# Two last rows of Y and Z per batch pair in one row-tiled product, made once for all eight batches

## The chip, the cores and the metric

The kernel runs on one core of one Trainium2 chip. The metric is device time in microseconds. TensorE (PE) multiplies, its weight loads are shown as PEld; VectorE is DVE, ScalarE is ACT, GpSimd is POOL, and SyncE is SP. SP, ACT and POOL also issue DMA transfers, which run on the core's 16 DMA engines: queue q0 carries what POOL issues, q1 what SP issues, q10 what ACT issues.

## The reference

Sliding-window attention (8 batches, 8 heads, 576 positions of 64 dimensions, window 64) gives x with 576 rows and 512 columns per batch. Then, per batch:

```python
X = np.fft.rfft(x, axis=1)
Xr, Xi = (np.real(X[:, :n_modes]), np.imag(X[:, :n_modes]))      # 64 modes
Yr = np.einsum('bmd,mde->bme', Xr, w_r) - np.einsum('bmd,mde->bme', Xi, w_i)
Yi = np.einsum('bmd,mde->bme', Xr, w_i) + np.einsum('bmd,mde->bme', Xi, w_r)
Y[:, :n_modes] = Yr + 1j * Yi
y = np.fft.irfft(Y, n=S, axis=1)
u = x + y
return (u + np.maximum(u @ w_ch, 0.0)).astype(np.float32)
```

w_r and w_i have 64 matrices of 512 x 512 each, together 128 MiB in fp32. They are read once.

## The kernel before, in words

**Stages.** POOL issues the loads of q, k, v and of the weights (L165, cast to bf16 on the way, 1 MB as landed). Attention runs under the first half of the weight loads, the products of modes with weights (`mode_half`, L188) under all of them. A group of four modes has four weight loads: two halves of the 512 inputs (hb), each with w_r and w_i (ri). The list `steps` sets their order. The modes of groups LAST = 12 and 13, which give rows 96 to 111 of Y (`rows`, L591, 16 of 128 rows: real and imaginary part of eight modes), come last.

**What is done with Y.** With T the inverse transform as a matrix (`trigI` in bf16, `trigIr` in fp32r, 128 rows of Y by 576 positions), u = x + T Y. The second part is u w_ch = x w_ch + T (Y w_ch) = x w_ch + T Z. The products x w_ch are made under the loads, one per tile of 128 positions, and kept as `XW[i]` (L756). A finished group goes through `finish_group`: `turn` (L648) transposes its staged rows into YT (the tile Yall, seen as transposed). `batch_job(b)` turns that round into rows of Y (`yrows`, tile Yall, ACT, L689) and multiplies it with w_ch into rows of Z (`multiply`, L610; ACT casts it into Zall, L693). Rows 96 to 111 are zero in both until the end.

**Tiles.** There are 36: four per batch of 128 positions each, and four "x4" tiles (8, 17, 26, 35), each of which holds the last 64 positions of two batches. For the 16 tiles of batches 0 to 3 (NLB = 4) `early_u` and `add_late` (L703, L704) add T Y and T Z of the 112 known rows under the loads, into UE[i] and XW[i]; only the 16 last rows remain for the tail. The others take all rows in the tail.

**The order of jobs under the last loads.** `batch_job`, `early_u` and `add_late` are put in one list. `advance` prepares one job and finishes the one before it. The variable `want` sets how many are advanced after each half step, and what is left is done before the last w_r and w_i products of the load stage (`half == n0+n1-2`).

**After the last landing** (L994 to L1023): the last group's rows are staged (`cast_halves`: DVE takes one half, ACT the other). `turn` transposes them; `put_first` (L656) puts the last rows of batches 0 to 3 into one PSUM bank, 32 partitions per batch, for the row-tiled products of the tail; `put_y` (L652) puts all rows of all batches in another. ACT copies `trz` (L663, the transposed rows of batches 0 to 3) and `trl` (L660, all of them). trz times w_ch in two halves (L1007) gives ZL, cast by DVE and ACT. trl times w_ch (L1015) gives the last rows of Z for all batches. Two DMAs carry the last rows into their places: Yall (L1011, from yst) and Zall (L1021, from zst).

**The tail.** `seq` lists pairs of tiles. A pair of early tiles takes `tail_xw` (L786, XW through an identity product), `late_u` (L796) and `late_z` (L803): products with only 16 rows, which sit in separate row groups of TensorE (tile_position), so that a pair's four run side by side. DVE adds into UE (L829), ACT applies the relu (L834), POOL adds both (L835). Other pairs take `full_u` (L845 adds x through an identity product, L849 or, for x4 tiles, L854 adds T Y) and `full_z` (L786, L868 adds T Z with all 128 rows; DVE takes relu and sum, L899). In `add_x` some tiles leave out L845: DVE adds x instead (L860), or POOL (L864). Results go out through SP (L821, in the order of `plan`) and ACT.

**The tables of the row-tiled products** (L950 to L952) are copies of the 16 last rows of trigI and trigIr into four row groups, eight DMAs on SP, made at the start of the second load stage.

```python
r = slice(YG[b], YG[b] + 16)
nc.tensor.matmul(out=pu[i], lhsT=trigL[r, at:at + 128], rhs=YL[r], start=True, stop=True,
                 tile_position=(YG[b], 0))
```

Of the kernel before, what the change touches and what calls it, by code (L numbers as in the profile page):

```python
# [26 lines left out]
def kernel(  # L27
# [39 lines left out]
    ident = consts.tile([128, 128], FP32, name="ident")  # L67
# [3 lines left out]
    pick = consts.tile([128, 32 * NLB + 8], BF16, name="pick")  # L71
# [125 lines left out]
    with tc.manual_schedule():  # L197
        maskp = pool("maskp")
        mask_t = maskp.tile([128, 2, 4, 128], BF16, name="mask_t")
# [221 lines left out]
        def trig_steps():  # L421
            yield lambda: ve.memset(trigF[64:128, NTC - 1, :], 0.0)
            yield lambda: ve.memset(trigF[0:64, NTC, :], 0.0)

            yield lambda: ve.tensor_copy(out=sel, in_=ident.rearrange("p (g x) -> p g x", x=32)[:, :, 0:16])
            yield lambda: ve.memset(pick, 0.0)
            yield lambda: zero_xq(1, ve)
            for to in range(0, NLB, 2):
                b = (to + 2) % NLB
                yield lambda to=to, b=b: ve.tensor_copy(  # L430
                    out=pick[:, 8:].rearrange("p (b x) -> p b x", b=NLB)[:, to:to + 2, 0:8].rearrange("p b (g r) -> p b g r", g=4),
                    in_=sel.rearrange("p g (r b) -> p b g r", b=B)[:, b:b + 2])
# [93 lines left out]
        trigL = zpool.tile([128, 4 * 128], BF16, name="trigL")  # L526
        trigLr = zpool.tile([128, 4 * 128], FP32R, name="trigLr")
        trl = zpool.tile([128, NDCH, 128], FP32R, name="trl")
        trz = zpool.tile([128, NDCH, NLB, 32], FP32R, name="trz")
# [3 lines left out]
        rowpool = pool("rowpool", reuse_waits="tile")  # L533
# [58 lines left out]
        YG, ZG = (64, 96, 0, 32), (0, 32, 64, 96)  # L592
# [37 lines left out]
        def finish_group(grp, psm):  # L630
            stg = stgpool.tile([128, DM], BF16, name="stg")
            if grp == LAST + 1:
                cast_halves(stg, psm)
            elif grp < EARLY:
                nc.vector.tensor_tensor(out=stg, in0=psm, in1=Yacc[grp], op=ALU.add)  # L635
            else:
                nc.vector.tensor_copy(out=stg, in_=psm)
            i = grp % 2
            end = grp - i == LAST
            if i == 0:  # L640
                late["pt"] = bank("p", [128, NDCH, 128])
                late["py"] = bank("y") if end else None
            pt, py = late["pt"], late["py"]
            lanes = sel.rearrange("p g x -> p (g x)")

            def turn():
                for c in range(NDCH):
                    nc.tensor.matmul(out=pt[:, c, 64 * i:64 * i + 64], lhsT=stg[:, 128 * c:128 * c + 128], rhs=lanes,  # L648
                                     start=True, stop=True)

            def put_y():
                nc.tensor.matmul(out=py[64 * i:64 * i + 64, :], lhsT=lanes, rhs=stg, start=True, stop=True,  # L652
                                 tile_position=(0, 64 * i))

            def put_first():
                nc.tensor.matmul(out=late["first"], lhsT=pick[:, 8 - 8 * i:136 - 8 * i], rhs=stg,  # L656
                                 start=(i == 0), stop=(i == 1))

            def take():
                nc.scalar.copy(out=trl[:, :, 64 * i:64 * i + 64], in_=pt[:, :, 64 * i:64 * i + 64])  # L660

            def take_first():
                nc.scalar.copy(out=trz[:, :, :, 8 * i:8 * i + 8],  # L663
                               in_=pt[:, :, 64 * i:64 * i + 64].rearrange("p c (r b) -> p c b r", b=B)[:, :, 0:NLB])

            def prepare():
                turn()
                if end:
                    put_y()
                    take_first()  # L670
                    take()
                elif i:
                    k0 = 8 * (grp - 1)
                    nc.scalar.copy(out=YT[:, :, :, k0:k0 + 16], in_=pt.rearrange("p c (k b) -> p b c k", b=B))

            if end:
                late[i] = turn, put_first, take, put_y, take_first
            if not (end and i):
                ready.append(prepare)
# [19 lines left out]
        def add_late(b, c):  # L699
            def done(_):  # L700
                i = tile_of(b, c)
                pz = bank("z")
                nc.tensor.matmul(out=pz, lhsT=trigIr[:, 128 * c:128 * c + 128], rhs=zrows(b), start=True, stop=True)  # L703
                nc.vector.tensor_tensor(out=XW[i], in0=pz, in1=XW[i].bitcast(FP32), op=ALU.add)  # L704

            jobs.append((lambda: None, done))
# [23 lines left out]
        def early_jobs(b):  # L730
            early_u(b, (1,))
            add_late(b, 0)
            early_u(b, (3,))
            add_late(b, 1)
            add_late(b, 2)
            early_u(b, (0, 2))
            add_late(b, 3)
# [25 lines left out]
        AA = [(18 * k // 2 + c, 18 * k // 2 + 4 + c) for k in range(NLB // 2) for c in range(4)]  # L763
# [28 lines left out]
        def late_u(n):  # L792
            for i in seq[n]:
                (at, b), = tiles[i][1]
                r = slice(YG[b], YG[b] + 16)
                nc.tensor.matmul(out=pu[i], lhsT=trigL[r, at:at + 128], rhs=YL[r], start=True, stop=True,  # L796
                                 tile_position=(YG[b], 0))

        def late_z(n):
            for i in seq[n]:  # L800
                (at, b), = tiles[i][1]
                r = slice(ZG[b], ZG[b] + 16)
                nc.tensor.matmul(out=ps[i], lhsT=trigLr[r, at:at + 128], rhs=ZL[r], start=False, stop=True,  # L803
                                 skip_group_check=True, tile_position=(ZG[b], 0))
# [34 lines left out]
        add_x = {X4[0][1]: "dve", X4[1][0]: "dve", X4[1][1]: "dve", BB[0][0]: "dve", BB[0][1]: "pool"}  # L839
# [26 lines left out]
        def rows_z(i):  # L866
            for at, b in tiles[i][1]:
                nc.tensor.matmul(out=ps[i], lhsT=trigIr[:, at:at + 128], rhs=zrows(b), start=False, stop=True,  # L868
                                 skip_group_check=True)
# [25 lines left out]
        def full_z(n):  # L895
            ut = uts[n]
            for j, i in enumerate(seq[n]):
                rows_z(i)
                nc.vector.scalar_tensor_tensor(out=ut[:, j], in0=ps[i], scalar=0.0, in1=ut[:, j],  # L899
                                               op0=ALU.max, op1=ALU.add)  # L900
                send(i, ut[:, j])
# [34 lines left out]
        for i, (grp, hb) in enumerate(steps[EARLY:]):  # L936
            f, l = grp < EARLY or hb == 0, hb == 1
            if i == EARLY:
                while tables:
                    tables.pop(0)()  # L940
                while jobs or pend:
# [6 lines left out]
                nc.vector.tensor_scalar(out=trz.rearrange("p c g k -> p c (g k)"), scalar1=0.0, scalar2=None, op0=ALU.mult,  # L948
                                        in0=ident.unsqueeze(1).to_broadcast([128, NDCH, 128]))
                for g in range(4):  # L950
                    nc.sync.dma_start(out=trigL[32 * g:32 * g + 16], in_=trigI[rows, 0:512])
                    nc.sync.dma_start(out=trigLr.bitcast(FP32)[32 * g:32 * g + 16], in_=trigIr.bitcast(FP32)[rows, 0:512])  # L952
# [3 lines left out]
            for ri in range(2):  # L956
# [16 lines left out]
                if l and ri:  # L973
                    finish_group(grp, psm)
                    if grp == NGRP - 1:
                        ready.pop(0)()
                        for b in range(B):
                            batch_job(b)
                            if 0 < b <= NLB:
                                early_jobs(b - 1)  # L980
                half += 1
# [4 lines left out]
                else:  # L986
                    want = NT - NX0 + (half - n0 - n1 + 8) * (B + 7 * NLB) * 2 // 11
# [6 lines left out]
        turn, put_first, take, put_y, take_first = late[1]  # L994
        tr, first = trl, late["first"]
        turn()
        take_first()
        put_first()
        put_y()
# [4 lines left out]
        zl = [bank("z"), bank("m")]  # L1004
# [4 lines left out]
        yst = rowpool.tile([128, DM], BF16, name="yst")  # L1009
        nc.scalar.copy(out=yst, in_=late["py"])  # L1010
        nc.sync.dma_start(out=Yall[rows], in_=yst)  # L1011
        cast_halves(ZL, zl)
        pz = bank("p")
        for c in range(NDCH):
            nc.tensor.matmul(out=pz, lhsT=tr[:, c, :], rhs=wch[:, c, :], start=(c == 0), stop=(c == NDCH - 1))  # L1015
        banks_u(0)
        late_u(0)
        late_z(0)
        zst = trpool.tile([128, NDCH, 128], FP32R, name="tr").rearrange("p c k -> p (c k)")
        nc.scalar.copy(out=zst, in_=pz)  # L1020
        nc.sync.dma_start(out=Zall.bitcast(FP32)[rows], in_=zst.bitcast(FP32))  # L1021
        take_u(0)
        take_z(0)  # L1023
        for n in range(1, len(seq) - 1):
# [40 lines left out]
```

## Time and profile before

| what | value |
|---|---|
| median of three runs | 435.41 us (435.04 to 435.62) |
| the profiled execution's own time | 435.39 us |
| its span | 433.6 us |
| PE busy | 327.2 us, 75% |
| DVE busy | 229.8 us, 53% |
| ACT busy | 180.1 us, 42% |
| POOL busy | 101.2 us, 23% |
| q0, software_dynamic | 81.73 MB, 99.7% of 16 engines' span |
| q1, hardware_dynamic | 9.77 MB, 6.6% |
| mean granted TensorE clock | 0.899 |

The span is the time from the first to the last instruction that the profile records. Busy time is the sum of an engine's instructions; TensorE's matmuls are pipelined, so that the start of one and the start of the next say more than the shown duration. Rows of the timeline read: start, microseconds, engine, line, operation, output<-inputs, shapes, count, and in brackets the idle time ahead of it and what ended it. Rows of the chain read: time, duration, engine, output, line.

### The profile page before, as it was taken

The numbers are of one execution on the slowest core, as the hardware profiler recorded it, in microseconds if no ns is written. First come the engines' busy times: TensorE is split into PE (matmuls) and PEld (weight loads), VectorE is DVE, ScalarE is ACT, GpSimd is POOL, SyncE is SP. The second block draws the span as 40 slices with busy tenths as digits, with TensorE's granted clock in tenths as the row PEclk, the third lists the DMA queues.
The fourth block names the chain that finished last, engine by engine and source line by source line (L and its number), as shares of the span: only waits on it lengthen the run. The fifth ranks groups of instructions, "written<-read, shape, count | busy, mean of one in ns | idle before, by whom it ended". The sixth has DMA issues, their size and how long they took to land.

```text
span 433.6 us, 11034 instructions
## 1 busy us (share of the span) xinstructions
PE 327.2 (75%) x4802; PEld 214.6 (49%) x4802; DVE 229.8 (53%) x472; ACT 180.1 (42%) x322; POOL 101.2 (23%) x150
## 2 busy tenths in 40 slices
PE   6999999998999999963208343767584668779993
PEld 3666667576667666641104121444353345445652
DVE  8588787876776776863104111122131325752994
ACT  5665757565666666520201100122121213434842
POOL 8322222222131231122102100012111112110990
PEclk8899999999999999996557768588889989999998
DMA  8999999999999999999999999999999999993798
GB/s 203 212 211 212 211 211 213 210 211 212 212 213 211 212 212 211 212 213 211 212 259 212 218 212 212 212 210 212 212 209 212 211 212 212 212 212 77 245 365 288
DMA packets 47280, 93.64 MB, mean 216 GB/s; under 512 B 2688, under 2 KB 3136, under 8 KB 47232
## 3 DMA queue, kind: packets, MB, share of 16 engines
q0 software_dynamic: 41008, 81.73, 99.7%
q1 hardware_dynamic: 5328, 9.77, 6.6%
q10 hardware_dynamic: 896, 1.44, 0.9%
q8 instruction: 37, 0.61, 0.5%
q14 instruction: 11, 0.09, 0.1%
HBM read 163.58 MB, written 9.44 MB: 399 GB/s over the span
## 4 chain that ended last, share of the span: by engine, by line
DMA 51%; PE 36%; issue 5%; ACT 3%; DVE 3%; POOL 1%; DVEq 0%; POOLq 0%
DMA wi<-in_moe_w_i_dram 29%; DMA wr<-in_moe_w_r_dram 22%; PE tr L231 6%; PE s L278 4%; PE s L270 3%; PE s L290 3%; PE pt L298 3%; PE psm L188 3%; PE vb L243 3%; PE o L318 2%; PE psz L786 1%; PE pst L786 1%; PE pst L868 1%; PE psz L610 1%; PE px L341 1%
## 5 line engine op out<-in xcount | busy, mean ns | idle before, releaser
L610 PE MATMUL psz<-wch,tr 128*128 128x512 f32 x176 | 62.3, 486 | 11.7 <-DMA wch<-in_moe_w_ch_dram 11.0
L756 DVE CAST xw<-psz 128x512 fp32r<-128x512 f32 x36 | 24.9, 692 | 86.1 <-PE psz L610 86.1
L584 ACT CAST tr<-ptx 128x512 fp32r<-128x512 bf16 x36 | 21.1, 586 | 104.1 <-PE ptx L603 104.1
L282 DVE TENSOR_REDUCE mx<-s 128x4 fp32r<-128x512 f32 x72 | 49.6, 688 | 27.0 <-PE s L278 26.7
L188 PEld LDWEIGHTS <-XQ 128*32 128x32 bf16 x448 | 18.8, 175 | 79.2 <-issue 55.9
L188 PE MATMUL psm<-wi,XQ 128*32 128x512 bf16 x208 | 20.1, 461 | 37.6 <-DMA wi<-in_moe_w_i_dram 37.6
L165 POOL DMA_DIRECT2D wi<-in_moe_w_i_dram x32 | 23.4, 732 | 102.8 <-PE psm L188 74.7
L610 PEld LDWEIGHTS psz<-wch,tr 128*128 128x128 f32 x176 | 36.8, 232 | 18.8 <-issue 11.5
L292 ACT ACTIVATE p<-s 128x512 bf16<-128x512 f32 x72 | 39.7, 603 | 12.9 <-PE s L290 12.9
L165 POOL DMA_DIRECT2D wr<-in_moe_w_r_dram x27 | 20.2, 749 | 97.0 <-PE psm L188 49.0
L188 PE MATMUL psm<-wr,XQ 128*32 128x512 bf16 x184 | 17.9, 465 | 28.3 <-DMA wr<-in_moe_w_r_dram 27.4
L235 ACT COPY kT<-tr 128x576 bf16<-128x576 bf16 x32 | 23.2, 724 | 21.1 <-PE tr L231 21.1
L278 PE MATMUL s<-kT,qT 64*64 64x128 bf16 (+1 forms) x576 | 29.2, 221 | 0.0
L270 PE MATMUL s<-mask_t,ident_bf 128*128 128x512 bf16 x72 | 28.4, 395 | 0.9 <-ACT p L292 0.8
L301 DVE COPY pts<-pt 128x1024 bf16<-128x1024 bf16 (+1 forms) x40 | 25.2, 629 | 5.0 <-PE pt L298 3.6
L235 ACT COPY qT<-tr 128x576 bf16<-128x576 bf16 x32 | 23.3, 728 | 10.6 <-PE tr L231 10.6
L278 PEld LDWEIGHTS <-qT 64*64 64x64 bf16 x576 | 17.8, 107 | 18.0 <-issue 17.5
L635 DVE TENSOR_TENSOR stg<-psm,Yfour 128x512 bf16<-128x512 f32 x10 | 6.9, 690 | 36.8 <-PE psm L188 36.8
L290 PE MATMUL s<-mx,ident_r 128*128 128x512 f32 x72 | 26.2, 437 | 0.0
L235 ACT COPY vT<-tr 128x576 bf16<-128x576 bf16 x32 | 23.3, 727 | 4.3 <-PE tr L231 4.2
L298 PE MATMUL pt<-ident_bf,p 128*128 128x128 bf16 x288 | 23.3, 220 | 1.7 <-issue 1.6
L218 POOL DMA_DIRECT2D rawk<-in_k_dram x15 | 8.1, 539 | 65.3 <-PE tr L231 59.1
(217 smaller groups left out, 607.4 us busy)
## 6 DMA issues: line engine op xcount, KB each, us to landing
wi<-in_moe_w_i_dram POOLq DMA_DIRECT2D x29, 1024.0 KB, 18.6
wr<-in_moe_w_r_dram POOLq DMA_DIRECT2D x27, 1024.0 KB, 17.9
out_dram<-ut SPq DMA_DIRECT2D x23, 256.0 KB, 2.8
rawv<-in_v_dram POOLq DMA_DIRECT2D x16, 288.0 KB, 15.0
rawk<-in_k_dram POOLq DMA_DIRECT2D x15, 288.0 KB, 14.1
rawq<-in_q_dram POOLq DMA_DIRECT2D x15, 288.0 KB, 14.0
x_sb<-in_moe_w_r_dram POOLq DMA_DIRECT2D x2, 1024.0 KB, 15.9
out_dram<-utx SPq DMA_DIRECT2D x5, 256.0 KB, 3.1
```

The costliest lines, as they stand in the source:

```text
L165: nc.gpsimd.dma_start(out=w[:, to:to + len(ps)], in_=src[ps[0]:ps[-1] + 1, HALF * hb:HALF * hb + HALF, :].rearrange("g (p j) e -> p g j e" ...
L188: nc.tensor.matmul(out=ps[32 * g:32 * g + 32, 0:e], lhsT=of.rearrange("k s b m -> k (s b) m")[:, (3 * j + 1 - ri) * B:(3 * j + 5 - ri) * B ...
L231: nc.tensor.transpose(out=pt[ro, j, :], in_=raw[ro, TH * half + j, :], identity=ident_bf[ro, ro])
L235: nc.scalar.copy(out=to, in_=pt.rearrange("p j n -> p n j"))
L270: nc.tensor.matmul(out=s, lhsT=ident_bf, rhs=mask_t[:, mk], start=True, stop=True)
L278: nc.tensor.matmul(out=s[ro, t, lo:128], lhsT=lq, rhs=kT[ro, 64 * n - 64 + lo:64 * n + 64], start=False, stop=True, skip_group_check=True)
L282: nc.vector.tensor_reduce(out=mx, in_=s, axis=AX.X, op=ALU.max, negate=True)
L290: nc.tensor.matmul(out=s, lhsT=ident_r, rhs=mx.unsqueeze(2).to_broadcast([128, 4, 128]), start=False, stop=True, skip_group_check=True)
L292: nc.scalar.activation(out=p[:, 4 * c2:4 * c2 + 4, :], in_=s, func=ACT_F.Exp, scale=EX_SCALE)
L298: nc.tensor.transpose(out=pt[:, t, :], in_=st[u]["p"][:, t, :], identity=ident_bf)
L301: nc.vector.tensor_copy(out=ps[:, 0:nt, :], in_=pt[:, 0:nt, :])
L610: nc.tensor.matmul(out=pz, lhsT=tr[:, c, :], rhs=wch[:, c, :], start=(c == 0), stop=(c == NDCH - 1))
```

## The change

- **Last rows for all batches at once.** `put_first` and `turn` now use `pick`, regrouped so that the 16 last rows of *two* batches lie in one group of 32 partitions (four groups for eight batches). One product group then gives YL and ZL for all eight batches. `put_y`, the copies trl and yst, the product L1015 and the cast zst go.
- **Row-tiled products of 32 rows.** trigL and trigLr get a second copy each, with zeros at the rows of the other batch (rows of the two batches alternate), so that a product over 32 rows gives one batch's part. Pairs of early tiles are now of batches b and b + 2, so that the two lie in different row groups.
- **Copies of the last rows.** Four Yall DMAs (two batches each) and two Zall DMAs (batches 4 to 7) from YL and ZL take the place of the two. The Zall rows of batches 0 to 3 stay zero, as nothing reads them after.
- **x4 tiles.** Their T Z of the 112 known rows is added to XW under the loads (four more `add_late`, each of two products). In the tail one product over 32 rows with `trigX`, whose 128 columns hold both batches' tables, adds the rest. Three of the four leave `add_x`: x comes through L845 again, and ACT, not DVE, copies the result.
- **Order after the last landing.** `late_u` of the first pair comes between the two halves of the trz product.
- **Tables.** The copies of trigL, trigLr and trigX are 24 DMAs on SP where there were 8; DVE clears trigL and trigLr first. `pick` is built by six small copies where there were two.

```diff
-            for to in range(0, NLB, 2):
...
+            to = pick[:, 16:].rearrange("p (n x) -> p n x", x=32)[:, :, 0:16]
+            for n in range(6):
+                yield lambda n=n: ve.tensor_copy(
+                    out=to[:, n].rearrange("p (g r b) -> p g r b", g=4, b=2),
+                    in_=sel.rearrange("p g (r n b) -> p n g r b", n=4, b=2)[:, n % 4])
...
-        trl = zpool.tile([128, NDCH, 128], FP32R, name="trl")
-        trz = zpool.tile([128, NDCH, NLB, 32], FP32R, name="trz")
+        trz = zpool.tile([128, NDCH, 4, 32], FP32R, name="trz")
+        trigX = zpool.tile([128, 128], FP32R, name="trigX")
...
+        def group_y(b):
+            return 32 * ((b // 2 + 2) % 4)
+
+        def group_z(b):
+            return 32 * (b // 2)
...
             def take():
-                nc.scalar.copy(out=trl[:, :, 64 * i:64 * i + 64], in_=pt[:, :, 64 * i:64 * i + 64])
-
-            def take_first():
-                nc.scalar.copy(out=trz[:, :, :, 8 * i:8 * i + 8],
-                               in_=pt[:, :, 64 * i:64 * i + 64].rearrange("p c (r b) -> p c b r", b=B)[:, :, 0:NLB])
+                nc.scalar.copy(out=trz[:, :, :, 16 * i:16 * i + 16],
+                               in_=pt[:, :, 64 * i:64 * i + 64].rearrange("p c (g x) -> p c g x", x=16))
...
+        def add_late(i):
             def done(_):
-                i = tile_of(b, c)
                 pz = bank("z")
-                nc.tensor.matmul(out=pz, lhsT=trigIr[:, 128 * c:128 * c + 128], rhs=zrows(b), start=True, stop=True)
+                for n, (at, b) in enumerate(tiles[i][1]):
+                    nc.tensor.matmul(out=pz, lhsT=trigIr[:, at:at + 128], rhs=zrows(b), start=(n == 0),
+                                     stop=(n == len(tiles[i][1]) - 1))
                 nc.vector.tensor_tensor(out=XW[i], in0=pz, in1=XW[i].bitcast(FP32), op=ALU.add)
...
-        AA = [(18 * k // 2 + c, 18 * k // 2 + 4 + c) for k in range(NLB // 2) for c in range(4)]
+        AA = [(tile_of(b, c), tile_of(b + 2, c)) for b in range(NLB // 2) for c in range(4)]
...
-                r = slice(ZG[b], ZG[b] + 16)
-                nc.tensor.matmul(out=ps[i], lhsT=trigLr[r, at:at + 128], rhs=ZL[r], start=False, stop=True,
-                                 skip_group_check=True, tile_position=(ZG[b], 0))
+                r = slice(group_z(b), group_z(b) + 32)
+                nc.tensor.matmul(out=ps[i], lhsT=trigLr[r, b % 2, at:at + 128], rhs=ZL[r], start=False, stop=True,
+                                 skip_group_check=True, tile_position=(group_z(b), 0))
...
-        add_x = {X4[0][1]: "dve", X4[1][0]: "dve", X4[1][1]: "dve", BB[0][0]: "dve", BB[0][1]: "pool"}
+        add_x = {BB[0][0]: "dve", BB[0][1]: "pool"}
...
         def rows_z(i):
-            for at, b in tiles[i][1]:
-                nc.tensor.matmul(out=ps[i], lhsT=trigIr[:, at:at + 128], rhs=zrows(b), start=False, stop=True,
-                                 skip_group_check=True)
+            at, b = tiles[i][1][0]
+            if len(tiles[i][1]) == 2:
+                r = slice(group_z(b), group_z(b) + 32)
+                nc.tensor.matmul(out=ps[i], lhsT=trigX[r], rhs=ZL[r], start=False, stop=True, skip_group_check=True,
+                                 tile_position=(group_z(b), 0))
+                return
...
-                nc.vector.tensor_scalar(out=trz.rearrange("p c g k -> p c (g k)"), scalar1=0.0, scalar2=None, op0=ALU.mult,
-                                        in0=ident.unsqueeze(1).to_broadcast([128, NDCH, 128]))
+                nc.vector.memset(trigL, 0.0)
+                nc.vector.memset(trigLr.bitcast(FP32), 0.0)
                 for g in range(4):
-                    nc.sync.dma_start(out=trigL[32 * g:32 * g + 16], in_=trigI[rows, 0:512])
-                    nc.sync.dma_start(out=trigLr.bitcast(FP32)[32 * g:32 * g + 16], in_=trigIr.bitcast(FP32)[rows, 0:512])
+                    for x in range(2):
+                        to = slice(32 * g + x, 32 * g + 32, 2)
+                        nc.sync.dma_start(out=trigL[to, x], in_=trigI[rows, 0:512])
+                        nc.sync.dma_start(out=trigLr.bitcast(FP32)[to, x], in_=trigIr.bitcast(FP32)[rows, 0:512])
+                        nc.sync.dma_start(out=trigX.bitcast(FP32)[to],
+                                          in_=trigIr.bitcast(FP32)[rows, 576 - 64 * x:704 - 64 * x])
...
                             if 0 < b <= NLB:
                                 early_jobs(b - 1)
+                            if b % 2:
+                                add_late(9 * (b // 2) + 8)
...
-                    want = NT - NX0 + (half - n0 - n1 + 8) * (B + 7 * NLB) * 2 // 11
+                    want = NT - NX0 + (half - n0 - n1 + 8) * (B + 7 * NLB + 4) * 2 // 11
...
+        zl = [bank("y"), bank("z")]
+        banks_u(0)
         for h, ps_ in enumerate(zl):
             for c in range(NDCH):
                 nc.tensor.matmul(out=ps_[:, 0:HALF], lhsT=trz[:, c].rearrange("p g k -> p (g k)"),
                                  rhs=wch[:, c, HALF * h:HALF * h + HALF], start=(c == 0), stop=(c == NDCH - 1))
-        yst = rowpool.tile([128, DM], BF16, name="yst")
-        nc.scalar.copy(out=yst, in_=late["py"])
-        nc.sync.dma_start(out=Yall[rows], in_=yst)
+            if h == 0:
+                late_u(0)
         cast_halves(ZL, zl)
-        pz = bank("p")
-        for c in range(NDCH):
-            nc.tensor.matmul(out=pz, lhsT=tr[:, c, :], rhs=wch[:, c, :], start=(c == 0), stop=(c == NDCH - 1))
-        banks_u(0)
-        late_u(0)
         late_z(0)
-        zst = trpool.tile([128, NDCH, 128], FP32R, name="tr").rearrange("p c k -> p (c k)")
-        nc.scalar.copy(out=zst, in_=pz)
-        nc.sync.dma_start(out=Zall.bitcast(FP32)[rows], in_=zst.bitcast(FP32))
+
+        def last_rows(gs):
+            for g in gs:
+                nc.sync.dma_start(out=Yall[rows, 2 * g:2 * g + 2], in_=YL[group_y(2 * g):group_y(2 * g) + 32])
+            for g in gs:
+                if 2 * g >= NLB:
+                    nc.sync.dma_start(out=Zall.bitcast(FP32)[rows, 2 * g:2 * g + 2],
+                                      in_=ZL.bitcast(FP32)[32 * g:32 * g + 32])
+
+        last_rows((2, 3))
         take_u(0)
         take_z(0)
+        last_rows((0, 1))
```

## The prediction

> **What bounds the kernel now.** I read the page first, then the chain of work that ended last, then the DMA view of three stretches, then the timeline of the two places the change touches. The profiled execution took 435.39 us, 0.02 below the median of the three runs (435.41), with a span of 433.6, so 1.8 us lie outside the span. I work against 435.39. About 0.2% of it, 0.87 us, is what a measurement of this kernel can tell from no change.
>
> ```profile
> DMA  8999999999999999999999999999999999993798
> GB/s 203 212 211 212 211 211 213 210 211 212 212 213 211 212 212 211 212 213 211 212 259 212 218 212 212 212 210 212 212 209 212 211 212 212 212 212 77 245 365 288
> ```
>
> The DMA engines are full in every slice up to the 37th, which is the end of the loads; then comes one gap, then the stores. So there are two stages: until about 396 us the weight stream decides, and whatever takes DMA time from it moves the end by that much. The chain says the same of the first stage, and names the waits around its end:
>
> ```profile
> 383.99 12.63 DMA wi<-in_moe_w_i_dram
> 396.66 0.50 PE psm L188 x3
> 397.18 0.43 DVE stg L627
> 398.50 0.68 PE psz L1007 x4
> 399.18 0.48 PE psm L1007 x4
> 399.66 0.93 PE psp L1015 x4
> 401.02 0.66 PE psz L786 x2
> ```
>
> From 396.66 on the chain is TensorE, one product after another. In the tail it is not alone (columns: PE, PEld, DVE, ACT and POOL busy, clock, DMA share, GB/s):
>
> ```profile
> 404.00:408.00 4.00, 4.00 (x27) 2.48 (x25) 3.67 (x8) 3.20 (x7) 4.00 (x4) 1.00 0.71 223
> 408.00:412.00 4.00, 4.00 (x23) 2.77 (x21) 3.35 (x7) 3.21 (x7) 4.00 (x5) 1.00 1.03 382
> 420.00:424.00 4.00, 4.00 (x25) 2.71 (x23) 3.90 (x7) 1.66 (x3) 2.93 (x3) 1.00 0.97 299
> ```
>
> PE and POOL have no gap, DVE little, and DMA stands at 1.03 from 408 us. A microsecond saved on one of them alone is not a microsecond saved.
>
> **Term 1: the tables copied under the loads.** Before, SP makes 8 small copies (L951, L952) of 16 rows each, 192 KB in all, between 230 and 243 us. After, it makes 24: 8 of trigL (16 KB), 8 of trigLr (32 KB), 8 of trigX (8 KB), 448 KB. What 8 cost is seen by comparing a stretch of 9.5 us with them and the next one without:
>
> ```profile
> q0 software_dynamic: 943, 1.87, 104.2%
> q1 hardware_dynamic: 256, 0.20, 8.3%
> ```
> ```profile
> q0 software_dynamic: 1015, 2.01, 112.3%
> ```
>
> q0 is the weight stream. With the copies beside it, it moved 1.87 MB instead of 2.01. 0.14 MB at 2.01/9.5 = 0.2116 MB per us is 0.66 us, near the 8.3% of 9.5 us (0.79) that the copies' packets took. The stream never runs dry after that (share 1.12 in every later stretch until 391), so the 0.66 us is still there at the last landing. Four more trigL and four more trigLr cost the same again, 0.66. The eight trigX cost between 64/192 of 0.66 (by bytes, 0.22) and 0.66 (by count); I take 0.42. Sum **+1.08** (0.88 to 1.32). Nothing waits for these tables until 400 us, and SP has nothing else to issue there. The Trainium skill, DMA: Bandwidth & Descriptors, section Anatomy of one DMA, prices a transfer at about 2 us fixed, mostly latency, plus its bytes at 436 GB/s. By it, as an estimate, the 256 KB more would take 0.60 us from the stream and the total below would be 0.5 lower; the stretch above shows more for fewer bytes, and I go by the stretch.
>
> The memsets of trigL and trigLr (DVE, same place) and the four more small casts for pick during attention replace or join DVE work while the stream decides: nothing. Their cover is the stream; a gap in the DMA row there would show it gone.
>
> **Term 2: four more add_late jobs under the last loads.** Each is two products on Zall rows and one DVE addition (0.68 us, row L704). The job after batch 5 and the job after batch 7 each wait for the Zall row that ACT has only just begun to cast. Before, TensorE goes on at once:
>
> ```profile
> 391.21 0.40 PE L688 MATMUL ptx<-ident_bf,Yall 128*128 128x128 bf16 x4
> 391.41 2.20 PE L610 MATMUL psz<-wch,tr 128*128 128x512 f32 x8
> 393.54 0.67 PE L188 MATMUL psm<-wr,XL 128*32 128x256 bf16 x16
> 394.15 0.39 PE L656 MATMUL psz<-stg,pick 128*128 128x512 bf16 x1
> 394.19 0.82 PE L786 MATMUL pst<-xw,ident_r 128*128 128x512 f32 x2
> 394.93 1.10 PE L188 MATMUL psm<-wi,XL 128*32 128x256 bf16 x12
> 396.66 0.60 PE L188 MATMUL psm<-wi,XL 128*32 128x256 bf16 x4 [0.62 <-DMA wi<-in_moe_w_i_dram]
> ```
>
> After (order of the changed program) this stretch, from the wi product at 387.98 to the wr product, holds: four wch products (1.01), four transposes (0.22), the tile-26 pair, four transposes, eight wch products (2.1), the tile-35 pair. The second product of a pair starts when the cast is done: last wch product's start + 0.4 + 0.14 + cast 0.62 + 0.17 to PE (from L610, L693 and the next waits). I get 390.09 for tile 26, 393.89 for tile 35, 394.27 for the wr product: 6.3 us where the rows show 5.57, **0.73** longer, although four early products and their wait for ACT (0.46) move ahead of 387.37. The stretch before that (376.66 to 381.74, 4.49 us, DVE without a gap) gets one wch group and one pair more: +0.95, of which the 1.17 us of waiting for wi at 387.37 swallows all but 0.28. So PE arrives 0.28 + 0.73 = 1.01 later at the last load, where it now waits 0.79 (from the last start at 395.76 plus 0.11; the row says 0.62 by a modelled end). Overshoot 0.22; I take **+0.25**, with bounds 0 (the waits are shorter, all is covered) and +1.0 (no slack at 387.37). This comes on top of term 1, since all landings shift together.
>
> **Term 3: from the last landing to the first store.** Removed: put_y (0.33 to the next start), L660, L1010, the product L1015 of all rows (399.49 to 400.52), the cast L1020 and the two 128-row copies to Yall and Zall. What L1015 did was also to cover ACT's cast of the second half (399.75, 0.37 us), on which late_z waits. After: the cast of trz has 256 elements instead of 128 (0.38 as L660, not 0.27), so L1007's first half starts at 398.55 (was 398.44); its last product starts at 399.02; then late_u(0) stands between the halves. A change between whole-array and row-tiled products costs TensorE: a full product is followed by the next after 0.23, by a tiled one after 0.33; the tiled pair (415.12) holds the next full product off until 415.54, 0.43. So late_u 399.24, second half 399.67, ACT's cast 400.52 to 400.89, late_z 401.06, next product 401.48. Before that was 400.95: **+0.53**, not a gain, because a wait takes the product's place. Bounds 0 (no change of mode is paid) and +0.6. POOL, whose sums run without a gap from 401.85 to 422.9, starts +0.38 later. Queued behind late_z are all of PE's tail products. 0.21 comes back at 405.57, where PE waited for the Zall copy: that copy now holds four batches in two transfers of 64 KB, issued near 401, so it lands before. SP's two extra Yall copies (0.6 each) go behind the first two stores, where SP waited 0.85 for POOL anyway. Net **+0.3**.
>
> **Term 4: the x4 tiles (two pairs).** Removed: per pair four Zall products (416.99 to 418.02), and three DVE additions (L860, 0.68 each). Added: two row-tiled products per pair with trigX, six ident products (0.11 each) and three ACT copies (0.59).
>
> ```profile
> 415.54 0.39 PE L845 MATMUL psm<-x,ident_bf 128*128 128x256 bf16 x2
> 415.87 0.62 PE L854 MATMUL psm<-Yall,trigI 128*64 128x512 bf16 x4
> 416.42 0.73 PE L786 MATMUL pst<-xw,ident_r 128*128 128x512 f32 x2
> 416.99 1.10 PE L868 MATMUL pst<-Zall,trigIr 128*128 128x512 f32 x4
> 418.02 0.41 PE L854 MATMUL psy<-Yall,trigI 128*64 128x512 bf16 x2
> ```
>
> With the starts of these rows and the two mode changes, pair one runs 415.54 to 417.73 (was 418.02) and pair two to 419.92 (was 420.08): **-0.15**. The added ident products and mode changes eat most of the 0.47 that four products less two side by side save per pair. DVE's sums can start 0.3 earlier, ACT's stores go about 1 us later behind the copies, and the hole in the stores at 420 to 424 (299 GB/s) closes a little or not: 0, with -0.7 and +0.4 as bounds.
>
> **Sum:** 1.08 + 0.25 + 0.3 - 0.15 = +1.48, so 435.39 + 1.48 = **436.9 us**.
>
> **Rivals.** (A) The stream makes the copies good, for example because half of the DMA rate is already gone from 391.5 us on (DMA share 0.75 and 140 GB/s in 390 to 395), so that the late packets fill idle engines: term 1 is 0 and the time 435.39 + 0.4 = 435.8, not told from no change. Against it: both stretches after the copies run at the same 2.01 MB, with nothing caught up. (B) PE under the last loads is worse: no slack at 387.37 and term 2 at +1.0, with term 3 at its upper end: 435.39 + 1.08 + 1.0 + 0.45 = 437.9. (C) Faster: the tail goes by PE's summed products. L1015 (1.03) and put_y (0.33) are gone, the pairs' four products become two side by side (0.94 to 0.24, twice: 1.4), less 0.66 for six ident products: -2.1. It decides once changes of mode cost nothing and ACT's cast is covered; with term 1 at its lower end and term 2 at 0, 435.39 + 0.88 - 2.1 = 434.2. The Trainium skill, TensorEngine Tiling (Array Packing), section Theoretical Speedup, speaks for C with up to 4 times for 32 rows; its section Key Properties, by which a mode switch drains the array, speaks against. The rows agree with the second (0.43 to the next full product, not 0.23). Also against C: DMA at 1.03 with 382 GB/s cannot take the stores 2 us earlier.
>
> **Chances.** Forecast 0.50, A 0.17, B 0.23, C 0.10. Faster by over 0.2%: C, 0.10. Within: A and a low end of the forecast, 0.19. Slower: 0.71. The range takes A in, and B with some of its upper side: 435.5 to 438.5.
>
> **What would show it.** Right: last wi landing about 1 us later; q0 at 1.87 MB per 9.5 us for three times as long after 234 us; PE waiting on ACT's Zall cast before two pairs near 390 and 394; late_z waiting for ACT's half cast with PE idle; the stretch from the last landing to the first L786 of the tail some 0.5 longer. Wrong: last landing unmoved (A), or the first POOL sum less than 5.2 us after the last wi product's start (C).

## The result and the profile after

The changed kernel takes 436.86 us (436.40 to 437.14, 7 runs), the kernel before 435.37 us (434.89 to 436.70, 7 runs) on the same chip: 1.0032 times as long, with a 95% interval of 1.0019 to 1.0044. The profiled execution took 436.63 us with a span of 434.7 us, against 435.39 and 433.6. That is 1.24 us between the two profiled executions and 1.49 between the medians.

The page of the changed kernel has the same two stages. Its DMA rows, to be laid beside those of before:

```profile
DMA  8999999999999999999999999999999999993698
GB/s 207 211 211 212 211 212 212 210 211 212 212 212 211 212 211 212 212 212 212 212 259 212 212 211 212 212 218 218 213 211 208 208 211 212 212 211 72 232 363 295
```

Slices 27 and 28 stand out at 218 GB/s: there are the copies of the tables, more bytes in all, while the share was at its limit already. They lie at 286 to 301 us, not at 230 to 243, since they wait for DVE to clear the tables first. What they took from the weights is seen in the DMA view of 283.5 to 303.5 us (queue, kind: packets, MB, share of 16 engines),

```profile
q0 software_dynamic: 1976, 3.92, 103.5%
q1 hardware_dynamic: 768, 0.46, 10.3%
```

and of the next 20 us, without copies:

```profile
q0 software_dynamic: 2120, 4.21, 111.8%
```

The weight stream moved 0.29 MB less, which is 1.4 us at 4.21/20 = 0.21 MB per us. The eight copies of before cost 0.66. So the change costs 0.7 to 0.8 us of stream here; the last packet of the weights ends at 397.24 us instead of 396.32, **0.92** later, 0.1 to 0.2 more than these rows give.

The timeline of TensorE under the last loads answers to the rows shown before:

```profile
390.84 1.12 PE L698 MATMUL psz<-Zall,trigIr 128*128 128x512 f32 x2
391.80 0.40 PE L683 MATMUL ptx<-ident_bf,Yall 128*128 128x128 bf16 x4
392.01 2.27 PE L615 MATMUL psz<-wch,tr 128*128 128x512 f32 x8
394.24 0.50 PE L698 MATMUL psz<-Zall,trigIr 128*128 128x512 f32 x1
394.95 0.50 PE L698 MATMUL psz<-Zall,trigIr 128*128 128x512 f32 x1 [0.21 <-ACT Zall L688]
395.39 0.67 PE L187 MATMUL psm<-wr,XL 128*32 128x256 bf16 x16
396.03 0.82 PE L782 MATMUL pst<-xw,ident_r 128*128 128x512 f32 x2
```

The wr products start at 395.39 instead of 393.54, late but still ahead of the last landing. The chain of work that ended last goes on from that landing:

```profile
386.31 11.20 DMA wi<-in_moe_w_i_dram
...
397.56 0.50 PE psm L187 x3
...
398.08 0.44 DVE stg L632
...
399.32 0.74 PE psy L1016 x4
400.06 0.32 PE psm L792 x2
400.38 0.68 PE psz L1016 x4
...
401.14 0.38 ACT tr L633
...
401.56 0.50 PE pst L799 x2
```

PE waits 0.29 us for the last weights at 397.56 (the products before start up to 397.16, and the next would follow 0.11 later), and then stands on ACT's cast (401.14) ahead of late_z (L799). From there the chain is PE to its end, as before.

### The profile page after: what moved, and what is told of

It is laid out like the page before. It is cut to its first block, busy times and chain, and to the rows that moved or that the text cites. A ratio compares the mean times of both kernels' runs of the same rounds, so it can differ in the third digit from the quotient of the medians.

```text
span 434.7 us, 11021 instructions
## 1 busy us (share of the span) xinstructions
PE 327.7 (75%) x4762; PEld 216.5 (50%) x4806; DVE 232.4 (53%) x478; ACT 180.6 (42%) x321; POOL 101.1 (23%) x150
## 3 DMA queue, kind: packets, MB, share of 16 engines
q10 hardware_dynamic: 896, 1.44, 1.0%
## 4 chain that ended last, share of the span: by engine, by line
DMA 46%; PE 37%; issue 6%; DVE 5%; ACT 3%; POOL 1%; DVEq 0%; POOLq 0%; ACTq 0%
DMA wi<-in_moe_w_i_dram 28%; DMA wr<-in_moe_w_r_dram 18%; PE tr L231 6%; PE s L278 4%; PE s L290 3%; PE pt L298 3%; PE psm L187 3%; PE vb L243 3%; PE psz L615 3%; PE o L318 2%; PE s L270 2%; DVE xw L700 2%; PE psz L782 1%; PE pst L782 1%; DVE XQ L718 1%
## 5 line engine op out<-in xcount | busy, mean ns | idle before, releaser
L615 PE MATMUL psz<-wch,tr 128*128 128x512 f32 x176 | 65.3, 506 | 11.6 <-DMA wch<-in_moe_w_ch_dram 11.0
L187 PE MATMUL psm<-wi,XQ 128*32 128x512 bf16 x208 | 21.3, 481 | 36.7 <-DMA wi<-in_moe_w_i_dram 36.7
L615 PEld LDWEIGHTS psz<-wch,tr 128*128 128x128 f32 x176 | 39.0, 245 | 19.7 <-issue 11.4
L187 PE MATMUL psm<-wr,XQ 128*32 128x512 bf16 x184 | 19.0, 488 | 25.7 <-DMA wr<-in_moe_w_r_dram 24.8
L330 DVE TENSOR_TENSOR x_sb<-o,r 128x512 bf16<-128x512 f32 x32 | 22.1, 692 | 1.1
```

The source lines that it names most:

```text
L187: nc.tensor.matmul(out=ps[32 * g:32 * g + 32, 0:e], lhsT=of.rearrange("k s b m -> k (s b) m")[:, (3 * j + 1 - ri) * B:(3 * j + 5 - ri) * B ...
```

## The experiments

Times are medians, set against the kernel before on the same chip ("+0.91" is the difference of the two medians; the changed kernel is +1.49). The end of the weights' last packet, POOL's first sum in the tail and SP's last issue are from each profiled execution.

| run | time, us | against before | weights end | first sum | last SP issue |
|---|---|---|---|---|---|
| before | 435.37 | | 396.32 | 401.85 | 428.57 |
| changed | 436.86 | +1.49 | 397.24 | 402.77 | 430.05 |
| e1 before, 24 copies | 436.06 | +0.91 | 397.18 | 402.70 | 429.48 |
| e3 before, no copies | 435.17 | +0.02 | 395.76 | 401.27 | 427.76 |
| e2 changed, no copies | 437.61 | +2.46 | 396.58 | 402.12 | 430.29 |
| e9 changed, no copies, SP issues x4 | 436.73 | +1.48 | 396.22 | 401.77 | 430.45 |
| e10 changed, SP issues x4 | 437.75 | +2.50 | 397.24 | 402.78 | 431.54 |
| e5 changed, x4 as before | 438.90 | +3.75 | 397.20 | 402.73 | 432.38 |
| e11 e5 with late copies | 442.79 | +7.54 | 397.35 | 404.35 | 436.78 |
| e14 changed, two more copies | 437.80 | +2.64 | 397.19 | 402.73 | 431.53 |
| e12 changed, Yall copies later | 437.67 | +2.42 | 397.49 | 403.04 | 431.75 |
| e15 changed, Yall copies first | 436.41 | +1.25 | 397.14 | 402.74 | 429.38 |
| e4 changed, late_u behind | 436.48 | +1.32 | 397.22 | 402.25 | 429.79 |
| e17 three costs removed | 437.70 | +2.67 | 395.81 | 400.82 | 430.56 |

The theory was that of the prediction: the copies under the loads cost about 1 us, and some tenths are lost between the last landing and the first store. The rivals were A (the stream makes the copies good), B (PE under the last loads) and C (the tail goes by PE's products).

**The copies.** e1 adds 16 copies, 256 KB, to the kernel before.

```diff
+                    nc.sync.dma_start(out=trigL[free], in_=trigI[rows, 0:512])
+                    nc.sync.dma_start(out=trigLr.bitcast(FP32)[free], in_=trigIr.bitcast(FP32)[rows, 0:512])
+                    for x in range(2):
+                        nc.sync.dma_start(out=trl.bitcast(FP32)[32 * g + 16 * x:32 * g + 16 * x + 16, 0],
+                                          in_=trigIr.bitcast(FP32)[rows, 0:128])
```

> The kernel before, with 16 more table copies on SP beside its 8 (4 of 16 KB, 4 of 32 KB, 8 of 8 KB, into partitions that nothing reads; the result is not touched). Theory (the weight stream pays for the copies): 24 copies take 1.42 us of the stream (0.30 MB at 0.2115 MB per us, from the trace of the changed kernel) where 8 took 0.66, so the last landing comes 0.76 to 0.9 us later and the time is 436.1 to 436.3, with nothing else of the change in it. Rival (the copies ride free and the change loses in the jobs under the loads or in the tail): 435.4.

Measured +0.91 (1.0023, 1.0012 to 1.0034), with the weights' end 0.86 later. Nothing else of the change is in this kernel. Rival A falls: the stream makes nothing good.

e2 takes the copies out of the changed kernel, e3 out of the kernel before. The tables are made by TensorE instead, with a matrix that selects the rows, and ACT casts them (five products in e2, two in e3):

```diff
-                    nc.sync.dma_start(out=trigL[to, x], in_=trigI[rows, 0:512])
...
+                    pq = bank("z")
+                    nc.tensor.matmul(out=pq, lhsT=s_[:, x], rhs=t[:, 0:512], start=True, stop=True)
+                    nc.scalar.copy(out=to[:, x], in_=pq)
```

> The changed kernel, with trigL, trigLr and trigX made by five products with a selection matrix on TensorE and ACT casts instead of 24 DMA copies. Theory: the stream gains 1.4 us, TensorE's chain under the last loads starts at a landing (352.9) and moves with it, so 435.3 to 435.6. Rival 1 (TensorE's chain under the last loads is a bound of its own, with 0.29 us left): only 0.3 us, 436.6. Rival 2 (the copies ride free): 436.9.

> The kernel before, its two tables made by two products on TensorE instead of 8 DMA copies. Theory: the stream gains 0.66 us, TensorE's wait at the last load (0.79) covers that, so 434.7. Rival (copies free): 435.4.

Both land earlier, e3 by 0.56 us against the kernel before, near its 0.66, and e2 by 0.66 against the changed kernel, less than half of its 1.4. Neither moves the time with it. e3 stands at +0.02 (0.9994 to 1.0013), and e2 is slower than the changed kernel, +2.46 (1.0045 to 1.0071).

The edit does one thing more, which the expectations left out. The table products stand on TensorE in front of the wr products near 282 us, and they wait for DVE's selection matrix (1.45 us in e2) and for ACT's casts. So these wr products start at 284.02 in e2, where they start at 281.09 in the changed kernel; POOL, which waits for them, issues the next weight load at 285.45 instead of 282.08, and the stream has a hole. It is widest in e9 below, which has e2's edit (windows: length, busy PE, PEld, DVE, ACT, POOL, clock, DMA share, GB/s):

```profile
286.00:288.00 2.00, 2.00 (x17) 1.11 (x18) 0.00 (x0) 0.82 (x3) 0.10 (x1) 0.50 0.82 154
288.00:290.00 2.00, 2.00 (x17) 1.03 (x15) 0.00 (x0) 1.07 (x3) 0.64 (x1) 0.50 0.72 123
```

From 280 to 300 us q0 moves 4.08 MB in e2, 4.09 in e3, 3.89 in e9 and 4.18 in e17. The kernel before, which has no copies there, moves 4.22, and the changed kernel with its 24 copies 3.96. At 0.21 MB per us, e2 loses by the hole 0.7 us of the 1.4 that it wins, e3 0.6 of its 0.66, and e9 1.6, more than it wins. The price of the copies can't be read from these kernels; e1 and the rows above give it.

e2's time is lost later. Up to 419 us e2's tail runs 0.67 us ahead; then ACT stands 3.15 us in one issue, that of its first half store of an x4 tile, where the changed kernel's took 0.56. e9 asks whether that issue is the loss, with SP issuing all half stores; e10 is the control without the other edit.

```diff
-        by_act = {(i, 1) for p in X4 for i in p} | {(p[1], 0) for p in BB[:-1]}
+        by_act = {(p[1], 0) for p in BB[:-1]}
```

> The changed kernel with its tables made by five TensorE products instead of 24 copies, and now with the second halves of the x4 tiles issued by SP, not by ACT. The same kernel with ACT's issues took 437.61 us although its last landing was 0.67 us earlier: ACT stood 3.15 us in its first issue of a half store at 419.6, the copy of the next tile, POOL, DVE and TensorE stood behind it. Theory (the lost time is that one issue on ACT): without it the tail is that of the changed kernel, 0.67 us earlier, so 436.0 to 436.4. Rival (the loss is in the stores themselves, half stores that move at half the rate whoever issues them): 437.3 to 437.8 again. Second rival (SP, with four more issues of 0.55 us each, is now the late one): 438 or more, with DVE or ACT waiting for stores.

> The changed kernel as it is, only with the second halves of the x4 tiles issued by SP instead of ACT: the control of the run beside it. Its ACT issues took 0.56 to 0.88 us and none stood long, so the theory (one long issue was the loss elsewhere) gives no change here: 436.6 to 437.1, ratio to the changed kernel 0.9995 to 1.0005. The rival (SP becomes the late one) gives 437.5 or more; if the half stores on ACT hold up ACT's copies even here, 436.0 to 436.4.

e9 came out 0.9 below e2, at 436.73: the long issue is gone, but the time is above what the theory gave. e10 gives one reason: four more issues on SP alone cost the changed kernel 1.0 us (SP's last issue at 431.54, not 430.05), where I had expected none. The hole is another. The two ran beside each other, and 437.75 - 436.73 = **1.02** with the same stores; the intervals (1.0020 to 1.0043 and 1.0047 to 1.0074) are apart, and the ends of the weights lie 1.02 apart too. That is not the copies' price once more, since e9's stream had won nothing by 300 us (3.89 MB moved from 280 us on, 3.95 in e10). It ends earlier because it runs at 209 GB/s from 392 to 394 us, where e10 has 138; why is open. What the pair shows is that a landing 1.02 us earlier can arrive at the end in full.

**The x4 tiles.** e5 undoes that part: all Z rows in the tail, DVE adds x, no `add_late` for these tiles. Their Zall rows must then be copied for all batches, four copies on SP behind the first pair instead of two.

```diff
-                if 2 * g >= NLB:
-                    nc.sync.dma_start(out=Zall.bitcast(FP32)[rows, 2 * g:2 * g + 2],
+                nc.sync.dma_start(out=Zall.bitcast(FP32)[rows, 2 * g:2 * g + 2],
...
-        add_x = {BB[0][0]: "dve", BB[0][1]: "pool"}
+        add_x = {X4[0][1]: "dve", X4[1][0]: "dve", X4[1][1]: "dve", BB[0][0]: "dve", BB[0][1]: "pool"}
```

> The changed kernel with its x4 tiles as before: no add_late for them under the loads, all 128 rows of Zall in the tail with four products per pair, x added by DVE for three of them, and last rows of Zall copied for all batches. Theory (stream decides, the jobs just fit): last landing unmoved, tail 0.1 to 0.2 longer by the products, DMA gets 128 KB more: 436.9 to 437.2. Rival (the four jobs under the loads hold up the last products): 0.3 to 1 us faster, 436.0 to 436.5.

+3.75, far from it. In its trace SP stands in the four copies from 405.7 to 409.1 us while finished tiles wait. e14 adds only the two Zall copies to the changed kernel (nothing reads them), e11 keeps e5 and spreads the four copies over the pairs 5 to 8, and e12 moves the changed kernel's two Yall copies to the same later place.

```diff
+            if n >= 4 and behind_rows:
+                put, g = behind_rows.pop(0)
+                put(g)
```

> The changed kernel with two more copies on SP behind the first pair of the tail: the last Zall rows of batches 0 to 3, which nothing reads afterwards. They stand at the place where the run with the x4 tiles as before (438.90 us) had them, and alone. Theory (there SP's four copies in a row were the loss, since finished tiles waited behind them while the DMA engines ran empty): the first store of a tile with all rows is issued near 409.1, not 407.27, and the time is 438.2 to 438.9, ratio to the kernel before 1.007 to 1.0085. Rival (the loss there was the x4 tiles themselves, that is four Zall products a pair and DVE adding x): no change, 436.7 to 437.1.

> The changed kernel with the x4 tiles as they were before (their Z rows with all 128 rows in the tail, DVE adds x, no add_late for them), as in the run that took 438.90 us, but its four copies of the last rows of batches 0 to 3 (two of Yall, two of Zall) are issued one by one behind the pairs 5 to 8 of the tail, not all four behind the first pair, where SP stood 3.4 us in them while finished tiles waited. Theory (those four issues on SP were the loss): 436.9 to 437.2, the changed kernel plus 0 to 0.3. Rival (the x4 tiles themselves cost 2 us when they have all rows and DVE adds x): 438.7 to 439.0 again.

> The changed kernel, only with its two copies of Yall's last rows of batches 0 to 3 moved from behind the first pair (405.7 to 407.2 on SP, just as the first tiles with all rows are finished) to behind the pairs 5 and 6. Theory (SP's order matters in the first microseconds, because from 408 us on the stores fill the DMA engines and their start sets their end): 0.3 to 0.6 us less than the changed kernel, 436.3 to 436.6. Rival (the end goes by the tail's engines, the copies only fill a gap): 436.8 to 437.0.

e14: +2.64, so two copies of 64 KB each, which nobody reads, cost 1.15 us more at this place, half of what e5 lost. The rival "no change" falls; the size given is missed, as is the first store with all rows (408.44, not 409.1). How a late issue becomes a late tail is in e14's chain:

```profile
412.51 0.59 SPq L817
...
413.20 3.03 DMA out_dram<-ut
...
416.33 0.58 ACT ut L858
```

A store issued late lands late, its `ut` buffer (there are seven) comes free late, and ACT, which needs the buffer for the next pair, holds up everything behind. The product that PE starts at 417.69 in the changed kernel starts at 418.57 here. Of the other half of e5's loss, 1.1 us, 0.68 lies in SP's queue as well: one of its four issues took 1.44 us instead of 0.58, and the first store with all rows went at 409.12, not 408.44. If such a delay arrives in full, as it did in e14 (1.17 us there, 1.15 in time), 0.4 us are left for the x4 tiles themselves; no run separates them.

e11 says nothing on that: the clock granted to TensorE fell to half at 399 us and stayed there for 14 us (windows as above).

```profile
406.00:410.00 4.00, 4.00 (x15) 1.51 (x14) 2.82 (x6) 2.41 (x6) 4.00 (x4) 0.50 0.54 197
410.00:414.00 4.00, 4.00 (x16) 2.65 (x15) 1.89 (x4) 1.54 (x4) 4.00 (x4) 0.61 0.19 70
```

All four runs of it lie between 442.64 and 443.09. No other kernel shows a clock under 1.00 between 360 and 428 us.

e12 came out the wrong way round: +2.42, not 0.3 to 0.6 below the changed kernel. The copies now stand at 410.97 to 412.2, in the middle of the saturated stretch; the stores of 408 to 416 run at 328 and 309 GB/s instead of 354 and 379. 0.26 us of it is a later landing that this edit doesn't explain. e15 goes the other way, into the 1.2 us in which SP has nothing to do ahead of the first store:

```diff
         last_rows((2, 3))
+        last_rows((0, 1))
         take_u(0)
         take_z(0)
-        last_rows((0, 1))
```

> The changed kernel with its two copies of Yall's last rows of batches 0 to 3 ahead of the first store, not behind the first pair's: SP has 1.2 us without work there, between 402.8 and 404.07, and two issues take 0.6 each. Theory (a copy costs only where finished tiles wait behind it in SP's queue): the first store of a tile with all rows goes at about 406.7, not 407.27, and the time falls by 0.3 to 0.6, to 436.2 to 436.6. Rival (these two copies filled a gap of the stores anyway): 436.7 to 437.0. Second rival (their 64 KB or SP's issues hold up the Zall copies, on which the second pair's products wait): 437.1 or more, with TensorE waiting for a DMA near 406.5.

The first store with all rows goes at 406.53, not 407.27, and SP's last issue 0.67 earlier, as the theory says. Of the time, +1.25 against +1.49 is left (1.0013 to 1.0034): less than expected, and not apart from the changed kernel's interval.

**The order after the last landing.** e4:

```diff
-            if h == 0:
-                late_u(0)
+        late_u(0)
         cast_halves(ZL, zl)
```

> The changed kernel with the first pair's row-tiled product late_u behind both halves of the trz product, not between them. One change from whole-array to row-tiled products and back goes from the path: the second half starts where the first one's next product is due, so ACT's cast and late_z come 0.5 us earlier (101.0 of the way: late_z at 401.0 to 401.1, not 401.56), late_u itself runs while ACT casts. Theory of the prediction's third step (that place cost up to 0.5 us at the first tail product): the first sum of POOL at 402.2 to 402.4, not 402.77, and the time 436.3 to 436.6. Rival (POOL's first sum waits for DVE's sum behind late_u, or the stores' start is set elsewhere): 436.7 to 437.0.

late_z at 401.03 instead of 401.56, POOL's first sum at 402.25 instead of 402.77. So the place of late_u costs 0.5 us at the first tail product, by the product itself and its change of mode together, as the step has it. The time: +1.32 (1.0017 to 1.0035), again little of it.

**Everything together.** e17 is e2 with e4's and e15's edits.

> The changed kernel with the three costs that the other runs named taken away together: the tables made by TensorE instead of 24 copies, late_u of the first pair behind both halves of the trz product, and the two Yall copies ahead of the first store. Theory (they add): last landing near 396.9 (0.67 us before the changed kernel's), the first sum of POOL near 401.6, and 436.86 - 0.67 - 0.38 - 0.45 = 435.36, so 435.1 to 435.7, no longer slower than the kernel before by what can be told. Rival (what is won ahead of the stores is lost in the drain, as where the tables alone were made by TensorE: ACT stands some 3 us in its first issue of a half store): 436.4 to 437.2.

The rival's mechanism came, and cost more than its range: 437.70, +2.67 (1.0045 to 1.0072), though POOL's first sum comes at 400.82, 1.95 us ahead of the changed kernel's. ACT's timeline shows the long issue again:

```profile
418.22 0.59 ACT L858 COPY ut<-psp 128x512 f32<-128x512 f32 x1
418.29 3.76 ACTq L817 DMA_DIRECT2D out_dram<-ut  x2
422.16 0.59 ACT L858 COPY utx<-psm 128x512 f32<-128x512 f32 x1 [3.35 <-PE psz L869]
```

The idle time is put down to PE, which had long been done; ACT stood in its own DMA issues, 3.11 us in the first. Behind it the next tile's copy, POOL, DVE, PE and SP's next store wait, and the stores fall to 177 GB/s:

```profile
420.00:424.00 4.00, 3.57 (x20) 1.99 (x18) 1.69 (x3) 1.18 (x3) 1.90 (x2) 1.00 0.72 177
```

The sum in this expectation was also too hopeful: 0.38 and 0.45 are differences of bare times from different chips. Against the kernel before on its own chip, e4 won 0.17 and e15 0.24.

## Why the prediction was right, step by step

The forecast was 436.9, measured 436.86, and part of that agreement is luck. The terms as measured on PE's chain add up to 0.90 + 0 + 0.07 - 0.16 = 0.81, not 1.48. The rest was lost in the drain, the last microseconds in which only stores run, and stood in no term.

- **Term 1, +1.08.** Right in kind and nearly in size: 0.92 at the last packet, and 0.91 in time for e1's 16 copies alone. The place was wrong (286, not 230 us), which changes nothing, since the stream is full in both. The price by bytes and count was somewhat high: 24 copies cost 1.4 us, three times the count but only twice the price of eight. The Trainium skill, DMA: Bandwidth & Descriptors, Anatomy of one DMA, whose fit is for DMAs that GpSimd issues, would price the 448 KB by its rate at about 1.05 us of stream, as an estimate. The row shows 1.4 for these copies, which SP issues.
- **Term 2, +0.25.** Too high: 0. PE's delay was read well as a whole (wr products worked out at 394.27 + 0.28 and term 1's 1.08, 395.63; measured 395.39), and one pair, not two, waited for ACT's cast. But its two parts came out as 0.72 and 0.24, not 0.28 and 0.73, and the 0.28 does not follow from the 0.95 and 1.17 that are given for it. PE still waits 0.29 us for the last wi, since from the start of the wr products to the last start ahead of that wait it takes 1.77 us where it took 2.22. The cover held, by a third of what it was.
- **Term 3, +0.53 at the first product, +0.3 net.** With the 0.90 of the last landing taken off, the first L782 starts at 401.10, 0.15 later than before, and POOL's first sum 0.02 later, so the sign "some 0.5 longer" did not come. In the steady part the shift is 0.07 (in the chain, the identity products of the sixth pair: 407.27, 406.30 before). The mechanism is as told (0.52 us of PE idle on ACT's cast), but three pieces were some 0.12 us shorter each: the start of the first half (398.42 with the 0.90 taken off, not 398.55), the change from tiled to whole products (0.31, not 0.43) and the step from the start of ACT's cast to late_z (0.42, not 0.54). Here a sentence failed: SP's two Yall copies "go behind the first two stores, where SP waited 0.85 for POOL anyway". They took 1.45 us there, and e14 shows what two more such issues cost at this place. I had priced them at nothing; e15, which moves these two away, gives back 0.24, which can't be told from no change.
- **Term 4, -0.15.** Right: with starts from the timeline, PE's L845 of the pair after the x4 tiles comes 0.81 later (420.89, 420.08 before) where the steady part is 0.97 later: -0.16.
- **The end.** The last store's issue is 1.48 later than before (430.05 against 428.57) and the span 1.1 longer, where PE's shift is 0.8. These 0.3 to 0.7 us in the drain were in no term. ACT now waits 1.1 us for `ut` and 1.1 us for `utx` buffers whose stores have not landed; which part is SP's copies and which the ACT issues that come later, the runs do not separate.
- **The rivals.** A fell with e1. B's mechanism (PE under the last loads) did not come: PE still waits. C's conditions did not hold: the row-tiled product cost 0.31 us and PE stood 0.52 on ACT's cast. Whether the stores could have taken an earlier start is less clear than the 382 GB/s made it: e4's start 0.5 us earlier hardly reached the end, e17's was swallowed by ACT's long issue, and e9's arrived in full.

One picture fits most runs: what delays the start of the tail or SP's queue arrives at the end in full or nearly so (e1, e10, e12, e14), what brings the start forward arrives hardly (e3, e4, e15) or turns round (e2, e17). e9 against e10 is an exception, and e3 half of one: in its profiled execution, the fastest of its eleven at 434.78 us, the span is 0.6 us shorter than before's, while its median did not move. No version beat the kernel before beyond what can be told; e3 equals it.

## What to carry to other kernels

A small copy beside a saturated load stream isn't hidden by having no reader: its price is the stream's, read from the stretch with it against the stretch without. When a stage is a drain of stores, look at the queue that issues them: a copy of 0.6 us on it can cost that much where finished tiles wait behind it, as in e14. Test an edit that shortens the way to a saturated stage down to the last store, not only to where its own step ends. And when an edit is to take one cost away, read the rows at the place of the edit for a new one: here the products that replaced the copies opened a hole in the very stream that they were to relieve.

## What the runs showed of the hardware

- One DMA issue on ACT, of a half store of 128 KB, stood 3.15 us (e2) and 3.11 us (e17), where the same issue took 0.56 in the changed kernel. In both, ACT's issue began 17 to 33 ns after SP's issue of a second half store, and it ended when SP's queue was nearly empty. In e4, e15 and before, it began with SP's first, or 0.37 us after it, and did not stand. Why is open.
- Stores of half the partitions are slow when nothing runs beside them: in e17 from 422 to 424.5 us only ACT's queue moved data, 92 to 98 KB per half us with the engines 0.89 to 0.97 busy, where stores of all 128 rows made 186 KB in the same run from 417 us on.
- In e11 TensorE lost half its clock at 399 us, after a stretch in which it was busy 0.39 to 0.83 of each us from 395 to 400, and stayed there some 14 us. e5, the same up to there with 0.48 to 0.81, kept 1.00. The Trainium skill, TensorE: Matmul & The Clock Gate, What's actually happening, lets the clock halve after an idle window of about 3.4 us and return after 3.4 us of activity. Here it halved without such a gap, and rows that are busy 3.48 to 4.00 of each 4 us from 402 us on did not bring it back before 412. How near the other kernels are to this, the rows do not say: from 394 to 398 us PE is busy 3.69 of 4 us in the changed kernel, 2.88 in e5 and 2.48 in e3, from 398 to 402 us 2.83, 2.83 and 4.00, and all three keep the full clock.
